# Moving one block of the output projection behind the last attention rows in a decode kernel

## The chip, the core and the metric

The kernel runs on one core of a Trainium2 chip. The metric is the device time of one execution in microseconds (us); the span is the part of it that the profile covers, from the first to the last instruction, and is 1.7 to 2.1 us shorter in nearly all runs here. PE is the TensorE matmul, PEld its weight load, DVE the VectorE, ACT the ScalarE, SPq the queue that issues the loads. SBUF is the on-chip memory that the loads fill, PSUM the memory that the matmuls write. A landing is the moment at which a load's data is there; the granted clock is the share of TensorE's full clock that the profile shows. Ratios are the mean time of one kernel's fast runs over that of the other's of the same rounds, so they are not quite the ratio of the medians that are quoted.

## The reference

A decode step: layernorm, attention of one query per sequence over the last 2048 cached positions with 32 heads of 192, output projection with residual, then a second layernorm and a GeGLU feed-forward with residual.

```python
# B=2, D=640, 32 heads, Dh=192, window W=2048 of 8192, F=1536; bf16
q = layernorm(x) @ wq
k, v = k_cache[:, :, -W:], v_cache[:, :, -W:]
p = softmax(q @ k^T * Dh**-0.5)
h = x + (p @ v).reshape(B, 1, 32*192) @ wo
n = layernorm(h)
out = h + (gelu(n @ w_gate) * (n @ w_up)) @ w_down
```

## The kernel before

One stream of loads runs through a ring buffer in SBUF: keys, values, output weights in four blocks of eight heads, then gate, up and down weights. The down weights come in four pieces of 4, 4, 2 and 2 blocks of 128 rows.

```python
WDC = ((0, 4), (4, 8), (8, 10), (10, 12))     # pieces of the down weights
...
        load_wo(2)
        load_wo(3)
        load_ffn()                            # wg, wu, then the pieces of wd
        pump()
```

The attention works in 16 groups of four heads of one sequence. For a group, `pv` multiplies probabilities by values into a PSUM bank, ACT copies it to `osb`, and `o_rows` gathers it into rows in another bank, `m1`. When four groups (eight heads of both sequences) are there, `o_spread` divides by the softmax sum on DVE, `o_columns` turns rows into columns, and `oproj(J)` multiplies by block J of the output weights and adds to `hT`. Blocks 2 and 3 are left for the end. In the trace PE runs its instructions in the order written here: `oproj(2)` from 273.69 us, `o_rows` of the last group from 276.12.

```python
        def oproj(J):
            wo, wtoks = where["wo", J]
            def fn(e):
                for kk in range(12):
                    for c in range(NC5):      # 60 weight loads, 60 matmuls of 2 columns
                        ins = e.matmul(m2[:, 32 + 2 * c:34 + 2 * c], lhsT=wo[:, kk, c:D:NC5],
                                       rhs=ot[:, J % 2, kk, :], ...)
            pe(fn, R=wtoks + [("ot", J % 2)], X=["m2"])
            ...                               # DVE: hT = m2[:, 32:42] + hT
        for g in range(NG):
            ...
            pv(g)
            if nxt:
                scores(g + 1)
            if not nxt:
                oproj(2)                      # heads 16 to 23
            o_rows(g)
            ...
            if g == NG - 2:
                o_spread(0, 96, 0)
        o_spread(96, 128, 4)
        o_columns(3)                          # heads 24 to 31
        oproj(3)
        layernorm(hT, "hT", hnT, "hnT")
        ...                                   # gate matmuls, gelu, up matmuls, down matmuls
```

`X=["m2"]` marks the PSUM bank that `o_columns`, `oproj` and DVE's readers share: PE waits there until DVE has read the bank's previous result.

## Time and profile before

| | before |
|---|---|
| time, median of 3 | 298.16 us (298.10 to 298.48) |
| span of the profiled run | 296.4 us |
| bytes loaded | 122.3 MB, 413 GB/s over the span |
| PE busy | 74% |

The page of the kernel before, sections 2 and 4: the busy share of 40 slices of the span in tenths (DMA busy, then GB/s) and the chain of work that ended last.

```profile
DMA  7999999999999999999999999999999999999981
GB/s 282 436 448 420 425 425 423 437 431 433 438 403 443 428 423 430 434 430 431 425 425 426 431 425 437 427 431 427 434 423 431 427 431 423 434 416 428 427 358 43
DMA 69%; PE 23%; ACT 3%; DVE 3%; issue 1%; SPq 1%
```

The DMA engines are 90% or more busy from the second slice to the thirty-eighth and move 403 to 448 GB/s there, in 32 of the 37 slices 423 to 438; 69% of the chain is DMA. So the loads set the pace. Only in the first slice and the last two is their share lower.

The chain of waits of the kernel before, its last 53 us (start, length, what; short pieces left out).

```profile
244.48 29.16 DMA ring<-in_A_wo_dram
...
273.69 2.57 PE m L609 x60
276.26 1.49 PE m L580 x4
...
279.50 0.88 PE m L597 x12
...
280.64 2.57 PE m L609 x60
...
286.28 2.15 PE sps L665 x60
...
288.81 2.11 PE ops L665 x60
...
291.18 1.10 PE m L696 x20
292.27 0.48 issue
292.75 0.97 PE m L696 x19
...
293.75 0.32 DVE yrow L702
```

L609 is `oproj`, L580 `o_rows`, L597 `o_columns`, L665 the gate and then the up matmuls, L696 the down matmuls. The chain's last wait for a load is that for output weights of heads 16 to 23 at 273.65. From there PE is the chain: everything after it, `o_rows` included, stands behind `oproj(2)`. Near the end the chain has a piece called "issue": PE stands still and the profile shows nothing that it waits for.

The timeline of the kernel before around two places (start, length, engine, line, operation, count, and in brackets the idle time before with what ended it).

```profile
271.97 0.49 ACT L573 ACTIVATE osb<-ops 128x384 f32<-128x384 f32 x1 [6.01 <-PE ops L566]
273.69 2.57 PE L609 MATMUL m<-ot,ring 128*128 128x2 bf16 x60 [1.77 <-DMA ring<-in_A_wo_dram]
276.12 1.63 PE L580 MATMUL m<-osb,selw 128*128 128x192 f32 x4
...
291.17 0.76 PEld L696 LDWEIGHTS m<-ring,uT 128*2 128x2 bf16 x28 [0.36 <-DVE uT L319]
292.76 0.61 PEld L696 LDWEIGHTS m<-ring,uT 128*2 128x2 bf16 x20 [0.82 <-issue]
```

First place: `osb` is complete at 272.46 and PE is idle for 1.77 us until 273.69, though `o_rows` could run. Second place: the pause comes after the 28th of 48 weight loads and lasts 0.82 us there (0.48 us between the modelled ends of the matmuls). The trace's records of landings, in us from the span's start: heads 16 to 23 at 273.65, heads 24 to 31 at 278.25, gate 282.94, up 287.55, the pieces of the down weights 289.08, 290.63, 291.45 and 292.23. No piece lands at 292.76, and the 28th weight load lies in the middle of the second piece, so the pause is no wait for a landing.

### The profile page before, as it was taken

The numbers are of one execution on the slowest core, as the hardware profiler recorded it, in microseconds if no ns is written. First come the engines' busy times: TensorE is split into PE (matmuls) and PEld (weight loads), VectorE is DVE, ScalarE is ACT, GpSimd is POOL, SyncE is SP. The second block draws the span as 40 slices with busy tenths as digits, with TensorE's granted clock in tenths as the row PEclk, the third lists the DMA queues.
The fourth block names the chain that finished last, engine by engine and source line by source line (L and its number), as shares of the span: only waits on it lengthen the run. The fifth ranks groups of instructions, "written<-read, shape, count | busy, mean of one in ns | idle before, by whom it ended". The sixth has DMA issues, their size and how long they took to land.

```text
span 296.4 us, 5662 instructions
## 1 busy us (share of the span) xinstructions
PE 218.2 (74%) x2537; PEld 173.7 (59%) x2537; DVE 125.4 (42%) x295; ACT 104.9 (35%) x138; POOL 1.0 (0%) x17
## 2 busy tenths in 40 slices
PE   2563459969795399988493699986787985874775
PEld 1551227839493386865382686673757783841764
DVE  5640286624364151644254243562454471451221
ACT  2150307534453061744161242653343463440000
POOL 1000000000000000000000000000000000000000
PEclk9996569996979587999788597999795999795555
DMA  7999999999999999999999999999999999999981
GB/s 282 436 448 420 425 425 423 437 431 433 438 403 443 428 423 430 434 430 431 425 425 426 431 425 437 427 431 427 434 423 431 427 431 423 434 416 428 427 358 43
DMA packets 6522, 122.63 MB, mean 414 GB/s; under 512 B 738, under 2 KB 740, under 8 KB 1252
## 3 DMA queue, kind: packets, MB, share of 16 engines
q1 hardware_dynamic: 6488, 122.29, 96.7%
q8 instruction: 19, 0.31, 0.4%
q14 instruction: 3, 0.02, 0.0%
q10 hardware_dynamic: 12, 0.00, 0.0%
HBM read 122.29 MB, written 0.00 MB: 413 GB/s over the span
## 4 chain that ended last, share of the span: by engine, by line
DMA 69%; PE 23%; ACT 3%; DVE 3%; issue 1%; SPq 1%
DMA ring<-in_A_k_cache_dram 42%; PE tps L466 12%; DMA ring<-in_A_wo_dram 10%; DMA ring<-in_A_wq_dram 9%; DMA ring<-in_A_v_cache_dram 8%; PE m L609 3%; ACT ktr L475 2%; PE ops L566 1%; ACT qrow L496 1%; DVE rq L319 1%; PE m L597 1%; PE sps L529 1%; PE sps L665 1%; PE ops L665 1%; PE m L696 1%
## 5 line engine op out<-in xcount | busy, mean ns | idle before, releaser
L466 PE MATMUL tps<-identf,ring 128*128 128x128 f32 x768 | 111.0, 310 | 40.2 <-DMA ring<-in_A_k_cache_dram 39.2
L466 PEld LDWEIGHTS tps<-identf,ring 128*128 128x128 f32 x768 | 101.8, 162 | 43.7 <-DMA ring<-in_A_k_cache_dram 40.4
L475 ACT ACTIVATE ktr<-tps 128x1024 bf16<-128x1024 bf16 x80 | 79.2, 1023 | 77.4 <-PE tps L466 76.9
L478 DVE COPY ktr<-tps 128x1024 bf16<-128x1024 bf16 x112 | 74.4, 688 | 60.7 <-PE tps L466 59.5
L535 DVE TENSOR_REDUCE mx<-sps 128x1 f32<-128x512 f32 x16 | 11.1, 692 | 47.5 <-PE sps L529 47.5
L566 PE MATMUL ops<-ring,ering 128*8 128x384 bf16 x512 | 25.9, 348 | 6.9 <-DMA ring<-in_A_v_cache_dram 6.7
L543 ACT ACTIVATE eexp<-sps,nm 128x512 bf16<-128x512 f32 x16 | 11.0, 687 | 52.8 <-DVE nm L541 50.0
L529 PE MATMUL sps<-ktr,rq 128*16 128x512 bf16 x384 | 27.7, 426 | 0.0
L566 PEld LDWEIGHTS ops<-ring,ering 128*8 128x8 bf16 x512 | 11.5, 89 | 16.7 <-DMA ring<-in_A_v_cache_dram 5.7
L529 PEld LDWEIGHTS sps<-ktr,rq 128*16 128x16 bf16 x384 | 10.5, 96 | 12.7 <-issue 4.5
L573 ACT ACTIVATE osb<-ops 128x384 f32<-128x384 f32 x16 | 7.8, 491 | 21.5 <-PE ops L566 21.5
L580 PE MATMUL m<-osb,selw 128*128 128x192 f32 x64 | 15.4, 365 | 0.0
L580 PEld LDWEIGHTS m<-osb,selw 128*128 128x128 f32 x64 | 10.5, 197 | 7.1 <-issue 7.1
L609 PEld LDWEIGHTS m<-ot,ring 128*128 128x128 bf16 x240 | 10.1, 131 | 2.8 <-DMA ring<-in_A_wo_dram 2.5
L609 PE MATMUL m<-ot,ring 128*128 128x2 bf16 x240 | 10.2, 178 | 2.1 <-DMA ring<-in_A_wo_dram 1.8
L488 PE MATMUL tps<-ring,xnT 128*32 128x384 bf16 x80 | 5.7, 444 | 8.1 <-DMA ring<-in_A_wq_dram 6.9
L319 DVE TENSOR_TENSOR rq<-ops,mask 128x96 bf16<-128x96 f32 x16 | 2.7, 247 | 16.9 <-PE ops L509 16.9
L524 PE MATMUL sps<-mskr,mskl 128*16 128x512 bf16 x64 | 7.0, 425 | 3.8 <-DVE mskl L315 3.8
L488 PEld LDWEIGHTS tps<-ring,xnT 128*32 128x32 bf16 x80 | 2.4, 120 | 10.9 <-DMA ring<-in_A_wq_dram 7.9
L539 PE MATMUL m<-mrhs,pm 128*128 128x16 f32 x32 | 6.3, 273 | 2.6 <-DVE mrhs L315 1.1
L319 DVE TENSOR_TENSOR orow<-m,wm 128x1536 bf16<-128x1536 f32 (+2 forms) x5 | 8.0, 1598 | 0.2
L319 DVE TENSOR_TENSOR ering<-m,mask 128x256 bf16<-128x256 f32 x16 | 6.7, 418 | 2.0 <-PE m L551 1.9
(97 smaller groups left out, 90.8 us busy)
## 6 DMA issues: line engine op xcount, KB each, us to landing
ring<-in_A_k_cache_dram SPq DMA_DIRECT2D x16, 3072.0 KB, 27.9
ring<-in_A_v_cache_dram SPq DMA_DIRECT2D x16, 3072.0 KB, 29.1
ring<-in_A_wo_dram SPq DMA_DIRECT2D x4, 1920.0 KB, 31.3
ring<-in_A_wq_dram SPq DMA_DIRECT2D x2, 3072.0 KB, 21.0
ring<-in_B_w_gate_dram SPq DMA_DIRECT2D x1, 1920.0 KB, 35.3
ring<-in_B_w_up_dram SPq DMA_DIRECT2D x1, 1920.0 KB, 27.2
ring<-in_A_wq_dram SPq DMA_DIRECT2D x1, 1536.0 KB, 27.9
ring<-in_B_w_down_dram SPq DMA_DIRECT2D x2, 640.0 KB, 28.9
```

What stands on the lines that cost most here:

```text
L319: return lambda e: e.tensor_tensor(out=out, in0=a, in1=b, op=op)
L466: ins = e.transpose(tps[bi][:, 128 * u:128 * (u + 1)], kv[:, off:off + 128], identf[:, :])
L475: act(lambda e, dst=dst, bv=bv: e.activation(out=dst, in_=bv, func=ACT.Copy), W=[("kt", slot, n)], X=[("t", bi)])
L478: dve(lambda e, dst=dst, bv=bv: e.tensor_copy(dst, bv), W=[("kt", slot, n)], X=[("t", bi)])
L488: ins = e.matmul(tps[J][32 * r:32 * (r + 1), 0:384], lhsT=xnT[:, c, :], rhs=wq[:, c - c0, 1536 * J + 384 * r:1536 * J + 384 * (r + 1)], st ...
L529: ins = e.matmul(sps[32 * ch:32 * ch + 16, :], lhsT=rq[:, g, k, :], rhs=ktr[:, g % 2, k // 2, 1024 * ch + k % 2:1024 * (ch + 1):2], start= ...
L535: dve(lambda e: e.tensor_reduce(out=mx[:, :], in_=sps[:, :], axis=AX.X, op=ALU.max), W=["mx"], X=["s"])
L543: act(lambda e: e.activation(out=eexp[:, :], in_=sps[:, :], func=ACT.Exp, bias=nm[:, 0:1], scale=1.0, accum_out=zr[:, g % 2, :]), R=["nm"] ...
L566: ins = e.matmul(ops_[32 * r:32 * r + 8, 0:384], lhsT=ering[:, g % 2, t, :], rhs=vv[:, 384 * t:384 * (t + 1)], start=(t < 4), stop=(t >= 2 ...
L573: act(lambda e: e.activation(out=osb[:, :], in_=ops_[:, 0:384], func=ACT.Copy), W=["osb"], X=["o"])
L580: e.matmul(m1[:, 0:DH], lhsT=selw[:, tp, w:w + 128], rhs=osb[:, DH * tp:DH * (tp + 1)], start=(g % 4 == 0 and tp == 0), stop=(g % 4 == 3 a ...
L609: ins = e.matmul(m2[:, 32 + 2 * c:34 + 2 * c], lhsT=wo[:, kk, c:D:NC5], rhs=ot[:, J % 2, kk, :], start=(kk == 0 and c == 0), stop=(kk == 1 ...
```

## The change

The intent is to let `o_rows` of the last group run while PE waits for output weights, and to run the 2.57 us of `oproj(2)` while DVE spreads the rows.

```diff
@@ in the loop over groups
             if nxt:
                 scores(g + 1)
-            if not nxt:
-                oproj(2)
             o_rows(g)
@@ after the loop
         o_spread(96, 128, 4)
+        oproj(2)
         o_columns(3)
         oproj(3)
```

No instruction is added or removed, and no load changes place: the last one is issued by 262.7.

## The prediction

> **What bounds the kernel.** The stream of loads. The page's slices show the DMA engines at 90% or more in every slice but the first and the last two, with a mean of 414 GB/s; the chain of waits that ended last is 69% DMA and 23% PE. 122.6 MB must arrive whatever the order of the matmuls. [...]
>
> **The tail now** (timeline and DMA issues, us from the span's start). All loads have been issued by 262.7, so the change moves no transfer. They land one after the other: values of group 15 at 269.1, output weights of heads 16 to 23 at 273.65, of heads 24 to 31 at 278.25, gate weights 282.95, up weights 287.55, the four pieces of the down weights 289.1, 290.6, 291.45, 292.2. On PE: pv to 271.97, osb copied at 272.46, then idle until the output weights land; oproj(2) 273.69 to 276.26, o_rows to 277.96, DVE spreads until 279.44, o_columns to 280.4, oproj(3) 280.64 to 283.2, layernorm, gate matmuls 286.28, up matmuls 288.74, down matmuls 291.18 to 293.7 with a pause of 0.48 to 0.8 us in the middle, output written, end 296.4. The granted clock is 0.50 throughout.
>
> **What the change does.** Nothing is added or removed. o_rows no longer waits behind oproj(2): it fills the idle stretch, 272.5 to about 274.35 (same 1.84 us as now). DVE spreads (about 1.5 us) until 275.9, hidden behind oproj(2), which now runs 274.35 to 276.9 (2.57 us). One small wait becomes bare: o_columns writes the bank that the addition to hT reads, so it waits about 0.25 us for that. o_columns 277.2 to 278.05, copy, oproj(3) can start at 278.3, just when its weights have landed (278.25), not at 280.64: 2.3 us earlier.
>
> **How much reaches the end.** Layernorm output comes at about 283.9 instead of 286.25, after the gate weights (282.95). But the up matmuls then wait for weights that land at 287.55: they start at 287.6, not 288.74. So 1.2 of the 2.3 us is lost to the DMA there. Down matmuls could start at 290.05, but their last piece lands at 292.2; after that 8 matmuls of the last piece (some 0.5 us) and the copy remain. yrow should start at 292.8 instead of 293.75. Saving: about 0.9 us of span, limited by the arrival of the last load, not by the matmuls moved.
>
> **Prediction:** 297.3 us (298.16 less 0.9), range 296.8 to 298.2. Faster by over 2%: 0.01; within 2%: 0.97; slower by over 2%: 0.02.
>
> **What would show each step.** In the timeline, o_rows(15) starts at about 272.5, before oproj(2), which begins when o_rows ends and not at a landing; o_columns(3) starts just after hT is added; oproj(3) near 278.3; the chain of waits shows DMA of the output weights of the last heads or nothing before it, and then the up or the down weights as releasers in the feed-forward part, which now are in nobody's way. Landings stay within some 0.3 us.
>
> **What would make it wrong.** If the pause in the down matmuls is no landing but a fixed one (an instruction fetch, which the trace shows ending at 291.3), it could stay or grow, and the gain shrinks to nothing or, if it moves early, 1.1 us. If the clock in the tail is granted at 1.0, PE work shrinks and the landing bounds still hold. A landing that drifts by 1 us between executions would hide the effect.

## The result, and the profile after

| | before | after |
|---|---|---|
| time, median of 6 | 298.14 us (298.02 to 298.48) | 297.40 us (297.27 to 297.45) |
| ratio of fast runs | | 0.9974, interval 0.9961 to 0.9986 |
| span of the profiled run | 296.4 us | 295.3 us |

The medians differ by 0.74 us, 0.25%; the interval leaves out 1. The page after, the same lines.

```profile
DMA  7999999999999999999999999999999999999992
GB/s 273 434 443 428 436 429 425 425 423 432 433 423 439 429 432 422 429 425 426 426 429 425 443 429 435 428 423 425 433 426 432 432 426 432 423 429 426 418 389 78
DMA 68%; PE 25%; DVE 2%; ACT 2%; SPq 1%; issue 0%
```

The chain of waits after, its end.

```profile
263.44 28.69 DMA ring<-in_B_w_down_dram
292.13 0.04 issue
292.18 0.47 PE m L695 x8
292.64 0.02 issue
292.67 0.33 DVE yrow L701
```

The stream is as before, but the chain now ends on the landing of the last piece of the down weights at 292.13. The last landing is where it was (292.23 before). What shrank is the distance from it to the final copy `yrow`: 293.75 - 292.23 = 1.52 us before, 292.67 - 292.13 = 0.54 us after. This distance is used below, because it takes the drift of the stream from run to run out of the comparison. From 276.2 to the end of the matmuls the granted clock is 0.50 in the traces before and after, in e1 and in e2, so no difference there is one of clock.

The timeline after, in PE's order. The lines have moved by one: L664 is gate and up, L695 the down matmuls.

```profile
272.15 0.49 ACT L573 ACTIVATE osb<-ops 128x384 f32<-128x384 f32 x1 [5.02 <-PE ops L566]
272.70 0.92 PE L580 MATMUL m<-osb,selw 128*128 128x192 f32 x4 [0.60 <-ACT osb L573]
...
273.72 2.56 PE L609 MATMUL m<-ot,ring 128*128 128x2 bf16 x60
...
276.54 0.88 PE L597 MATMUL m<-selb,orow 128*128 128x2 bf16 x12 [0.27 <-DVE hT L319]
...
278.41 2.53 PE L609 MATMUL m<-ot,ring 128*128 128x2 bf16 x60 [0.99 <-DMA ring<-in_A_wo_dram]
...
284.03 2.16 PE L664 MATMUL sps<-hnT,ring 128*128 128x2 bf16 x60 [0.80 <-DVE hnT L319]
...
287.56 2.16 PE L664 MATMUL ops<-hnT,ring 128*128 128x2 bf16 x60 [1.00 <-DMA ring<-in_B_w_up_dram]
...
289.99 1.84 PE L695 MATMUL m<-ring,uT 128*2 128x160 bf16 x40 [0.27 <-DVE uT L319]
...
292.18 0.44 PE L695 MATMUL m<-ring,uT 128*2 128x160 bf16 x8 [0.34 <-DMA ring<-in_B_w_down_dram]
```

`oproj(3)` starts 2.23 us earlier (278.41, not 280.64), the gate matmuls 2.25 us earlier. The up matmuls start only 1.2 us earlier, because PE now waits 1.00 us for their weights. The copy comes 1.08 us earlier. And the "issue" pause is gone.

So there are two candidates for the gain. One is the order, which moved PE's chain from behind the last landing to in front of it. The other is the vanished pause, up to 0.8 us, about as much as the whole gain.

### The profile page after: what moved, and what is told of

It is laid out like the page before. It is cut to its first block, busy times and chain, and to the rows that moved or that the text cites. A ratio compares the mean times of both kernels' runs of the same rounds, so it can differ in the third digit from the quotient of the medians.

```text
span 295.3 us, 5662 instructions
## 1 busy us (share of the span) xinstructions
PE 219.8 (74%) x2537; PEld 175.8 (60%) x2537; DVE 125.2 (42%) x295; ACT 105.1 (36%) x138; POOL 1.0 (0%) x17
## 4 chain that ended last, share of the span: by engine, by line
DMA 68%; PE 25%; DVE 2%; ACT 2%; SPq 1%; issue 0%
DMA ring<-in_A_k_cache_dram 49%; PE tps L466 18%; DMA ring<-in_B_w_down_dram 10%; DMA ring<-in_A_wq_dram 9%; PE ops L566 2%; PE m L609 2%; PE sps L529 1%; ACT ktr L475 1%; ACT qrow L496 1%; DVE rq L319 1%; SPq L264 1%; PE m L597 1%; DVE mx L535 0%; PE sps L524 0%; PE m L539 0%
## 5 line engine op out<-in xcount | busy, mean ns | idle before, releaser
L466 PE MATMUL tps<-identf,ring 128*128 128x128 f32 x768 | 114.0, 317 | 41.5 <-DMA ring<-in_A_k_cache_dram 40.8
L466 PEld LDWEIGHTS tps<-identf,ring 128*128 128x128 f32 x768 | 105.8, 166 | 44.4 <-DMA ring<-in_A_k_cache_dram 42.0
L566 PE MATMUL ops<-ring,ering 128*8 128x384 bf16 x512 | 27.4, 362 | 4.6 <-DMA ring<-in_A_v_cache_dram 4.4
L529 PE MATMUL sps<-ktr,rq 128*16 128x512 bf16 x384 | 26.2, 408 | 0.0
L580 PE MATMUL m<-osb,selw 128*128 128x192 f32 x64 | 14.7, 352 | 0.6 <-ACT osb L573 0.6
L488 PE MATMUL tps<-ring,xnT 128*32 128x384 bf16 x80 | 5.0, 403 | 7.1 <-DMA ring<-in_A_wq_dram 5.9
L539 PEld LDWEIGHTS m<-mrhs,pm 128*128 128x128 f32 x32 | 5.0, 195 | 4.8 <-DVE mrhs L315 4.8
```

The lines of the kernel that those rows point to most:

```text
L466: ins = e.transpose(tps[bi][:, 128 * u:128 * (u + 1)], kv[:, off:off + 128], identf[:, :])
L529: ins = e.matmul(sps[32 * ch:32 * ch + 16, :], lhsT=rq[:, g, k, :], rhs=ktr[:, g % 2, k // 2, 1024 * ch + k % 2:1024 * (ch + 1):2], start= ...
L539: pe(lambda e: e.matmul(m2[:, 256:272], lhsT=pm[:, :], rhs=mrhs[:, :], start=True, stop=True), R=["pm", "mrhs"], X=["m2"])
L566: ins = e.matmul(ops_[32 * r:32 * r + 8, 0:384], lhsT=ering[:, g % 2, t, :], rhs=vv[:, 384 * t:384 * (t + 1)], start=(t < 4), stop=(t >= 2 ...
L580: e.matmul(m1[:, 0:DH], lhsT=selw[:, tp, w:w + 128], rhs=osb[:, DH * tp:DH * (tp + 1)], start=(g % 4 == 0 and tp == 0), stop=(g % 4 == 3 a ...
```

## The experiments

**Theory A.** The old kernel had two excesses over the last landing. The pause hangs on a place in PE's instruction stream (the guess: the instructions that come next are fetched late), and is a large part of the 0.7 us; the order alone gives the rest. After the change the last landing bounds the end, and the other 1.2 us gained on PE are lost there. **Rival B.** The whole gain is the order; the pause is a wait for a landing or belongs to a moment, and plays no part.

### e1 and e2: shift PE's program, old and new order

Both get 85 small matmuls after the first layernorm, where PE idles for 5.9 us. They change no result. Each is a weight load and a matmul, so every later PE instruction moves by 170 places.

```diff
         layernorm(xT, "xT", xnT, "xnT")
+        def _fill(e):
+            for _ in range(85):
+                ins = e.matmul(m1[:, 400:402], lhsT=identb[:, :], rhs=identb[:, 0:2], start=True, stop=True)
+            return ins
+        pe(_fill, R=["identb"], X=["m1"])
```

> The old order with 85 small matmuls (170 PE instructions) added after the first layernorm, where PE idles from 4.95 to 10.8 us. They cost nothing by themselves but shift every later PE instruction by 170 places in the program. Theory A (half or more of the change's 0.7 us came from the pause of 0.5 to 0.8 us in the old down matmuls, which is a late fetch of PE's next block of instructions at a fixed place of the program): the pause is gone, the down matmuls run 291.2 to 292.9 without a gap, span about 295.6, time about 297.5. Rival B (the whole gain comes from the order; the pause is a wait for a landing): the pause stays after the 28th weight load, time 298.1.

> The new order with the same 85 small matmuls. Both theories: no change against the new order, 297.4 us, because the last piece of the down weights lands at 292.1 and ends the last wait. Difference to e1: A says 0.1 to 0.4 us (what the order alone gives), B says 0.7 us.

Measured: e1 297.73 us (297.49 to 298.31, 5 runs; ratio to before 0.9983, interval 0.9971 to 0.9996), e2 297.39 us (297.06 to 298.00, 5 runs; 0.9973, 0.9960 to 0.9987), before in the same rounds 298.25 us. The timeline of e1, down matmuls (L703 here) and copy:

```profile
291.48 1.43 PEld L703 LDWEIGHTS m<-ring,uT 128*2 128x2 bf16 x48 [0.36 <-DVE uT L319]
291.48 1.77 PE L703 MATMUL m<-ring,uT 128*2 128x160 bf16 x48 [0.28 <-DVE uT L319]
293.30 0.33 DVE L709 CAST yrow<-m 98x160 bf16<-98x160 f32 x1 [1.88 <-PE m L703]
```

The old order without the pause: 48 weight loads in one piece. From the first down matmul to the copy it takes 293.30 - 291.48 = 1.82 us, against 293.75 - 291.18 = 2.57 us before. The last landing of this run is at 292.40, so the copy follows it by 0.90 us, against 1.52 before and 0.53 in e2. Of the 0.98 us by which the distance shrank, then, 0.62 us go with the pause and 0.36 us with the order. The medians of the times give 0.52 us from before to e1 and 0.34 us from e1 to e2, but single runs of e1 and e2 scatter by 0.8 and 0.9 us. The split is rough: the medians of the spans (296.3, 296.0 and 295.6, to 0.1 us) give 0.3 and 0.4 us, and counted from the landing at which PE's last stretch begins (273.65 before, 273.94 in e1) the copy of e1 comes 0.74 us sooner. So the pause is worth some 0.3 to 0.7 us of the gain, and the order the rest. Rival B expected the pause to stay and e1 at 298.1, and falls. The profiled run of e1 (298.31 us) is the slowest of its five, but by what lies outside the span (2.3 us, 1.7 to 1.9 in the others), not by its tail.

### e3 and e4: take the landings away

Up and down weights are not loaded, their matmuls read the gate weights. Both have the fill, so neither has the pause.

```diff
-            for key, w in (("wg", B_w_gate), ("wu", B_w_up)):
+            for key, w in (("wg", B_w_gate),):
...
-            ...                              # the four loads of the down weights
-        pe(ffn_in(ops_, "wu"), R=["hnT"] + where["wu"][1], X=["o"])
+        pe(ffn_in(ops_, "wg"), R=["hnT"] + where["wg"][1], X=["o"])
...                                           # down matmuls: first 2560 columns of the gate tile
```

> Old order with the fill, wrong on purpose: the up and down weights are not loaded, their matmuls read the gate weights. Loads end at 282.9, so nothing after the gate weights can wait for DMA. PE's chain is as in the old order: gate matmuls at 286.3, yrow at about 293.0, time 297.3 to 297.5, nearly unchanged though 3.84 MB are no longer loaded.

> New order with the fill and the same loads left out. If the rest of the 2.3 us gained on PE was lost to the landings of the up and down weights, it shows here in full: gate matmuls at 284.0, yrow at about 290.7, time 2.2 to 2.4 us below e3. If the order is worth only what was measured, 0.3 to 0.8 us below e3.

Measured: e3 297.62 us (297.47 to 297.71, 4 runs), e4 295.31 us (295.17 to 295.52, 4 runs). Both give wrong results. With 3.84 MB fewer to load, the old order is no faster than e1 with all loads (297.73): without the pause and without those landings it is still PE's chain that ends it. The new order gains 2.31 us over the old, the whole of what it saves on PE. With the landings present it gained 0.34 us (e1 to e2). The missing 2 us are therefore lost to the arrival of the up and down weights, as theory A and the prediction say.

### e5 and e9: move the pause by a known number of instructions

The same fill in the old order, with 8 and with 16 matmuls instead of 85.

```diff
-            for _ in range(85):
+            for _ in range(8):               # e5; 16 in e9
```

> Old order with 8 small matmuls (16 PE instructions, a weight load and a matmul each) after the first layernorm. If the pause in the down matmuls hangs on a place in the instruction stream (theory A), it moves 8 pairs earlier: after the 20th of 48 weight loads instead of the 28th, still 0.4 to 0.9 us long. If it belongs to a landing or to the time, it stays at the 28th. Time about 298.1 either way.

> Old order with 16 small matmuls (32 PE instructions). Theory A: the pause moves on to after the 12th of 48 weight loads, and since PE reaches that place 0.26 us earlier than in e5 and the block arrives when it did, it grows slightly; yrow about 1.5 us after the last landing as before. Theory B: at the 28th.

The timeline of e5 (two lines), then of e9, weight loads of the down matmuls:

```profile
291.28 0.49 PEld L703 LDWEIGHTS m<-ring,uT 128*2 128x2 bf16 x20 [0.36 <-DVE uT L319]
292.60 0.88 PEld L703 LDWEIGHTS m<-ring,uT 128*2 128x2 bf16 x28 [0.83 <-issue]
```

```profile
291.23 0.23 PEld L703 LDWEIGHTS m<-ring,uT 128*2 128x2 bf16 x12 [0.36 <-DVE uT L319]
292.29 1.15 PEld L703 LDWEIGHTS m<-ring,uT 128*2 128x2 bf16 x36 [0.84 <-issue]
```

The pause moves exactly as many pairs as were put in: after the 28th, the 20th, the 12th weight load. It is tied to the instruction stream, and to no landing and no moment. A fetch is the suspect because the trace has packets of 16,384 bytes on a queue that the page calls "instruction": 19 of them in the span of the kernel before, 20 after the change. That such a packet holds the instructions that PE comes to next is an assumption and not shown. How many pairs of weight load and matmul go with one packet is an estimate: after the change 89 weight loads have started before the first packet and 2529 before the twentieth, which makes 128.4 pairs a packet (81 to 164 from one packet to the next; the trace before gives 132.4). With 128 pairs taken as a block that ends at the pause (without a pause, at the same place of the program), one can look up when PE entered that block:

| run | enters the block | next fetch starts | PE goes on | entry to going on |
|---|---|---|---|---|
| before | 287.60 | 290.19 | 292.76 | 5.16 us |
| e5 | 287.44 | 290.16 | 292.60 | 5.16 us |
| e9 | 287.12 | 289.87 | 292.29 | 5.17 us |
| e6 (below) | 286.96 | 289.72 | 292.29 | 5.33 us |
| after | 285.35 | 288.16 | no pause | it gets there at 290.83, 5.48 us |

In e7 and e8 (below), which have no pause either, PE takes 5.57 and 5.74 us. In the four runs with a pause PE went on 5.16 to 5.33 us after entry. The fetch itself takes 1.0 to 1.1 us in the trace, and in all four it ends before PE stops: at 291.28 in the kernel before, where PE stops at 291.94. PE goes on 1.40 to 1.50 us after its end. What fills that time, no view shows. The old order ran the 128 pairs in 4.3 us (287.60 to the pause at 291.94) and then paused. The new order runs the same 128 pairs, but spends time within them waiting for up and down weights (1.00 us for the up weights), is through after 5.48 us, and does not pause. It also enters the block 2.25 us earlier. Without those waits a pause would have ended at 290.5 to 290.7 (an estimate: 285.35 plus 5.16 to 5.33), still before the last landing at 292.13. That a late fetch causes the pause is inferred from the moving place and the nearly constant interval, which rests on the estimated block; no run speeds up a fetch by itself, so it is not shown.

The times miss what was expected: e5 took 299.53 us (298.99 to 299.74, 4 runs), not 298.1, and e9 299.22 us (298.87 to 299.43, 4 runs). The spans are nearly unchanged (296.5 in both profiled runs), so the growth lies outside the span: time less span was 2.4 to 3.2 us in the runs of both, against 1.9 before. The trace has a further instruction fetch after the end of the span, at 298.71 in e5 and 298.16 in e9. They end at 299.96 and 299.11; the times of the two runs are 299.72 and 298.87, 0.24 us less. The profiled run of e1 has the like: a fetch of 8 KB that ends at 298.55, its time 298.31, again 0.24 us less. No other trace here has a fetch after the span. So in these three runs the time seems to end with the late fetch and not with the program.

### e8: does that extra microsecond hang on the program's length?

The new order with the fill of 8.

> New order with the 8 small matmuls of e5. In e5 the time outside the span grew from 1.95 to 3.2 us. If that hangs on the length of PE's program, it comes again here: span as in the new order, 295.3, with no pause in the down matmuls, but a time near 298.5. If it belongs to the late pause, the time is 297.4.

Measured: 297.20 us (297.13 to 297.34, 4 runs), spans 295.4 to 295.5, time less span 1.7 to 1.8, no pause, and the last block fetched at 291.55, before the end. A longer program alone does not cost the microsecond. Why e5 and e9 fetch a block so late and the kernel before, which has the same pause and no fetch after 290.19, does not, stays open.

### e6: how much slack does PE have now?

The new order with the projection behind the o columns.

```diff
-        oproj(2)
         o_columns(3)
+        oproj(2)
         oproj(3)
```

> New order, but the output projection of heads 16 to 23 after the last o columns rather than before: PE waits for the DVE spread, then o_columns near 275.4, oproj(2) near 276.4, oproj(3) near 279.2 instead of 278.4, gate matmuls near 284.8 instead of 284.0. If the last landings bound the end, the up matmuls still start at their landing, 287.5, and the time stays 297.4 within 0.2. If PE's chain bounds it, 298.2.

Measured: 297.48 us (297.29 to 297.90, 5 runs; ratio to before 0.9972, interval 0.9958 to 0.9985), the time of the new order. The starts were later than expected: `o_columns` at 275.99, `oproj(2)` at 277.17, `oproj(3)` at 279.99, gate matmuls at 285.64. My expectation forgot that `oproj(2)` shares bank `m2` with `o_columns` and must wait for DVE's copy of it, and `oproj(3)` for the addition. So the up matmuls missed their landing by 0.5 us (288.09), and still four of the five runs took 297.29 to 297.52. Only one run was traced. If the others started as it did, which is not shown, PE's chain has 1.6 us of slack at the gate matmuls after the change (285.64 against 284.03). The traced run was the slowest (297.90) and shows the pause again:

```profile
290.53 0.76 PEld L695 LDWEIGHTS m<-ring,uT 128*2 128x2 bf16 x27 [0.36 <-DVE uT L319]
292.29 0.62 PEld L695 LDWEIGHTS m<-ring,uT 128*2 128x2 bf16 x21 [1.00 <-issue]
```

Its copy starts 1.07 us after the last landing (293.28 against 292.21). Here PE enters the block at 286.96, 1.6 us later than in the new order, and the pause lasts beyond the last landing; so in this run the pause, not the landing, bounds the end. Whether the four faster runs had it is not known.

### e7: less work after the last landing

```diff
-WDC = ((0, 4), (4, 8), (8, 10), (10, 12))
+WDC = ((0, 4), (4, 8), (8, 11), (11, 12))
```

> New order with the down weights loaded in pieces of 4, 4, 3 and 1 blocks instead of 4, 4, 2 and 2. The bytes and the end of the stream (292.1) stay; after the last landing 4 matmuls remain, not 8. If the last landing bounds the end, 0.1 to 0.15 us less, at the edge of what the rounds resolve; the trace shows yrow starting 0.35 us after the landing instead of 0.5.

Measured: 297.34 us (297.11 to 297.50, 5 runs; ratio to before 0.9968, interval 0.9955 to 0.9980). The copy starts 0.40 us after the last landing (292.60 against 292.20), not 0.54. That is the expected step in the trace, but the times do not tell it from the new order (297.40, 0.9974). No version clearly beats the new order.

## Why the prediction was right

The predicted time was 297.3 us, the measured one 297.40, within 296.8 to 298.2. By its steps:

- `o_rows` fills the idle stretch: yes, at 272.70 (272.5 predicted). It took 1.03 us, not 1.84: the granted clock was 1.00 from 272.7 to 276.1 in this execution; in e2, with the clock at 0.50 there, it took 1.86 us. It makes no difference at the end, since e2's `oproj(3)` starts at 278.42 and the new order's at 278.41, both on the landing.
- `oproj(2)` hides the DVE spread, `o_columns` waits bare for the addition to `hT`: yes, 0.27 us of idle PE against 0.25 predicted.
- `oproj(3)` at its landing, 278.3: yes, 278.41, 2.23 us earlier.
- 1.2 of these 2.3 us are lost at the landing of the up weights: yes, the up matmuls start at 287.56 (287.6 predicted). e4 against e3 shows the 2.31 us whole once the landings are gone.
- The end is bound by the last landing: yes, the copy starts at 292.67 (292.8 predicted), 0.54 us after it.
- The saving of 0.9 us: 1.08 us at the copy and 1.1 us of span in the profiled runs, 0.74 us in the medians of the time. Of these 0.3 to 0.7 us go with the pause (e1).

What the prediction did not see is where its 0.9 us come from. It subtracted a bound (the last landing plus a little work) from a measured end that held the pause, and so booked the vanishing of the pause as a gain of the order. e1 shows that without the pause in the old kernel the order would have given about 0.2 to 0.4 us. The pause stood among the things that could make it wrong, with a suspicion, an instruction fetch, that fits the runs but is not shown by them. The argument that it would do no harm was missing, and there was some luck in that: PE enters the block before it 2.25 us earlier and takes 5.48 us over it, 0.15 to 0.3 us longer than the time after which PE went on in the runs with a pause (5.33 and 5.16). In the profiled run of e6, where PE enters that block 1.6 us later, the pause comes back and the time is 297.90 us.

## What to carry to other kernels

When the loads are the bound, time saved on an engine counts only up to the next landing (here 2.31 us on PE came to 0.34): list the landings of the last loads beside the engine's chain, and predict the end as the later of the two. A pause that the profile ascribes to nothing deserves a test before it is booked: shift the instruction stream by some harmless instructions in an idle stretch and see whether the pause moves with the count. To take the drift of a long stream out of differences under 1 us, measure from the last landing, not from the start.
